# A recurrent attention layer beside a long convolution on one core: who loads the convolution's keys, how far ahead its input is loaded, and in what pieces two weight blocks are fetched

## The chip, the cores and the metric

The kernel runs on one core of one Trainium2 chip. The metric is the device time of one execution in microseconds (us), as the median of several runs. The execution that the profile shows has its own time, given below beside its span.

## The reference

Two independent results are written side by side, each 2048 x 1024. All inputs are bfloat16.

```python
# A: attention over segments of 32 rows, with 8 memory rows that are carried on
mem = mem0                                       # [1, 8, 1024]
for s in range(64):
    h = concat([mem, x[:, 32*s:32*s + 32]], 1)   # 40 rows
    q, k, v = h @ Wq, h @ Wk, h @ Wv             # 32 heads of 128
    p = softmax(where(mask, q @ k^T * scale, -1e9))
    o = (p @ v) @ Wo
    mem = o[:, :8]                               # the next segment waits for this
    outs.append(o[:, 8:])
# B: a state-space layer as a long convolution
K = real(einsum(Cc, exp(dt*A*l), dt*Bc))         # [1024 channels, 2048 steps]
y = irfft(rfft(u padded) * rfft(K padded))[:2048]
b = y.astype(bfloat16) + u * Dskip
return concat([a, b], -1)
```

## The kernel before

The program has three parts in time. The first, up to about 450 us, makes the convolution kernel K and does the work of A that doesn't depend on the memory. K is written to a table Kd in DRAM, the transform of u (the u spectra) to Ud. The second part, from about 450 to 700 us, is the transform: the spectrum of K, its product with that of u, and the inverse. The third is the 64 segments of A, one after the other.

**Transform.** The loop over `b` from 0 to 15 (L1320 to L1357) has one round for each pair of a quarter of the channels (`dq`, 256 channels) and a quarter of the frequencies (`kc`). A round `b`, in the order of its instructions:

- `spectrum(b + 1)` on PE (L1060, 64 matmuls of 256 columns) multiplies the key tiles `KT` with the matrices `MF`. The key tiles for the first two quarters are loaded before the loop; those of the third and fourth (`KT2`) are the deferred ones. ACT copies part of the result (`odd`, L1220 to L1222, tile `osb_`).
- `pointwise(b)` on DVE (L1228 to L1239) combines it with the two tiles `uq` of the u spectrum into `Bt`.
- SyncE issues the loads of the `uq` tiles for round `b + 2` (L1034), then some deferred key loads out of the list `keys` (L1342), then matrices `MI` for the inverse (b below 4), and then, in some rounds, weight blocks of A that are to stay in SBUF (`resident`, 512 KB each).
- From `b` = 4 on, two inverses. `inverse(dq, c)` has 32 matmuls on PE (L1287), with `MI` or with a negated copy `mn` that ACT makes (L1255). ACT scales the result into `yb` (L1303), DVE computes `uu = uu * Dskip + yb` (L1306, L1307), where `uu` is a tile of the input u, and the result is stored by a DMA that ACT issues (L1308), one inverse later.

There are 32 inverses: 24 in the loop, 8 behind it. Each needs one tile `uu` of 128 KB. `load_inverse` issues its load on SyncE; `NIV` is how many inverses ahead that is. `inverses()` calls it after each inverse for the one `NIV` places later. The first `NIV` loads are issued in round 3. Behind the loop, eleven weight blocks, then four blocks for the segments' ring `wst`, then five further weight blocks are issued between the last eight inverses.

Each of SyncE, ACT and GpSimd issues its instructions in program order, DMAs among them. A DMA that has to wait for a buffer or for an earlier DMA holds up what is behind it on its engine.

**Deferred keys.** `load_k` (L995) gathers a key tile from rows of Kd in 31 DMAs. With `later` given, it only appends them to a list, on the queues `qs` in turns. For the two deferred tiles this makes 62 DMAs, mostly of 32 KB in rows of 512 bytes.

**Segments.** Each segment multiplies its 32 rows of state `hT` with all blocks of Wk, Wq, Wv (L365) and then Wo (L475). Most blocks are in SBUF. Twelve are streamed from DRAM copies (WD) in every segment through the four slots of the ring `wst`. Three blocks are kept in PSUM instead, whole or half: `load_kept` copies them there with DVE as 32-bit words (`words`, L292, tile `keep`), and `fetch` copies them back into the tile `arena` in every segment. The block ("k", 0, 7) is kept whole. Of ("q", 0, 7) and ("o", 15), listed in `HALF`, the second half is kept in PSUM, and the first half lies in SBUF (`a_half`, `Whalf`). `load_kept` is called for them within the first segment. In segment 0 the Wo blocks that aren't in SBUF yet are loaded when their turn comes (`unit`).

Of the kernel before, what the change touches and what calls it, by code (L numbers as in the profile page):

```python
# [10 lines left out]
BF16 = mybir.dt.bfloat16  # L11
# [21 lines left out]
SLOTS = 4  # L33
# [199 lines left out]
def part_a(ctx, tc, x, src, WD, HE, seg_len, out_a, ahead, W_res, rest, places, first):  # L233
    nc = tc.nc
# [18 lines left out]
    wst = ahead.wst  # L253
    wres = ctx_w.enter_context(tc.tile_pool(name="a_wres", bufs=1, side="right"))

    loads = [SLOTS]
# [22 lines left out]
    kept, ahead_of, halves = {}, {}, {}  # L279
# [11 lines left out]
    def words(out, in_):  # L291
        nc.vector.tensor_scalar(out=out.bitcast(I32), in0=in_.bitcast(I32), scalar1=0, scalar2=None, op0=ALU.bitwise_or)  # L292

    def stage(key, in_):
        t_ = wst.tile([128, 2048], BF16, name="wst", tag="w%d" % (loads[0] % SLOTS))
        loads[0] += 1
        nc.sync.dma_start(out=t_[:].rearrange("e (h d) -> e h d", h=2) if len(in_.shape) == 3 else t_[:], in_=in_)
        return t_

    def load_kept(key):  # L300
        t_ = first.pop(key) if key in first else stage(key, src(key))
        kept[key] = {}
        for n in (1,) if key in HALF else (0, 1):
            kept[key][n] = ps_k.tile([128, 512], F32, name="keep", tag="keep%d" % sum(len(b) for b in kept.values()))
            words(kept[key][n][:], t_[:, 1024 * n:1024 * n + 1024])
        if key in HALF:
            t_ = ahead.low["half"] if key[0] == "q" else wres.tile([128, 1024], BF16, name="Whalf")
            nc.sync.dma_start(out=t_[:], in_=src(key)[:, 0, :] if key[0] == "o" else src(key)[:, 0:1024])
            halves[key] = [(0, 1024, t_)]

    def fetch(key):

# [334 lines left out]
def part_b(ctx, tc, u, A_re, A_im, B_re, B_im, C_re, C_im, log_dt, Dskip, out_b, ahead, copies, residents, first_state):  # L647
    nc = tc.nc
# [4 lines left out]
    DH, DQ = 512, 256  # L653
    v, sc, gp, pe, sy = nc.vector, nc.scalar, nc.gpsimd, nc.tensor, nc.sync
# [30 lines left out]
    with tc.tile_pool(name="b_par", bufs=1) as par, tc.tile_pool(name="b_parh", bufs=2) as parh, tc.tile_pool(name="b_mg", bufs=2) as mg, \  # L685
# [84 lines left out]
        o = 0  # L770
# [224 lines left out]
    def load_k(d0, n_d, qs, KT, later=None):  # L995
        dsl = slice(d0, d0 + n_d)

        def rows(r0, n, step=1):
            return Kd[r0:r0 + step * (n - 1) + 1:step, dsl]
        n_q = [0]  # L1000

        def get(out, in_):
            q = qs[n_q[0] % len(qs)]
            n_q[0] += 1
            if later is None:
                q.dma_start(out=out, in_=in_)
            else:
                later.append(lambda: q.dma_start(out=out, in_=in_))
        for r in (0, 2, 1, 3):
            k0 = KT[:, 4 * r, :]  # L1010
            get(k0[0:64], rows(r, 64, 4))
            get(k0[64:128], rows(256 + (0, 0, 1, 2)[r], 64, 2))
            k1 = KT[:, 4 * r + 1, :]
            if r == 2:
                get(k1[0:128:2], rows(384, 64, 2))
                get(k1[1:128:2], rows(386, 64, 2))
            else:
                get(k1[:], rows(384 + (0, 0, 0, 1)[r], 128))
            for mc in (2, 3):
                k2 = KT[:, 4 * r + mc, :]  # L1020
                q0 = 512 + 64 * (mc - 2)
                get(k2[0:128:2], rows(q0, 64))
                if r == 0:
                    get(k2[1:128:4], rows(q0, 32, 2))
                    get(k2[3:128:4], rows(q0 + 2, 32, 2))
                else:
                    get(k2[1:128:2], rows(q0 + 1, 64))
        return KT
# [20 lines left out]
    def spectrum(b, s_):  # L1049
        dq, kc = b // 4, b % 4  # L1050
        KN = KNs[dq // 2]
        d = slice(DQ * (dq % 2), DQ * (dq % 2) + DQ)
        KT = ks[0][:, :, d] if dq < 2 else ks[dq - 1][:]
        for half in range(2):
            for r in range(2):
                for cs in range(2):
                    for i, rr in enumerate((r, r + 2)):
                        for mc in range(4):
                            rhs = KN[:, 4 * (rr - 2) + mc, d] if half == 1 and i == 1 else KT[:, 4 * rr + mc, :]
                            pe.matmul(s_[r][half][:, cs, :], lhsT=MF[:, kc, 4 * rr + mc, cs, :], rhs=rhs,  # L1060
                                      start=(i == 0 and mc == 0), stop=(i == 1 and mc == 3), skip_group_check=True)
# [101 lines left out]
    for f in range(-1, 17):  # L1163
        if f == 15:
# [4 lines left out]
            ks = [load_k(0, DH, (sy, gp), ahead.pool.tile([128, 16, DH], BF16, name="KT", tag="kst"))]  # L1169
        if f == 16:  # L1170
            spectra = [load_u(0), load_u(1)]
        for word in ORDER:
            nm, r = word.rstrip("'"), f - word.endswith("'")
            if f == 16 and word == ORDER[0]:
                s0 = ps_e.tile([128, 2, 512], F32, name="pa", tag="pa")
                s1 = [ps_t.tile([128, 512], F32, name="ptt", tag="ptt") for _ in range(2)]
                first = [[s0[:, half, :].rearrange("p (c d) -> p c d", c=2) for half in range(2)],
                         [t_[:].rearrange("p (c d) -> p c d", c=2) for t_ in s1]]
# [25 lines left out]
    iv = ctx.enter_context(tc.tile_pool(name="b_iv", bufs=2))  # L1204
# [9 lines left out]
    KT2 = [pool.tile([128, 16, DQ], BF16, name="KT", tag="KT%d" % i) for i in range(2)]  # L1214
# [23 lines left out]
        for j, op in ((0, ALU.add), (1, ALU.subtract)):  # L1238
            v.tensor_tensor(out=Bt[:, kc, j], in0=Y[:, 0], in1=Y[:, 1], op=op)  # L1239

    NIV = 3
    unsent = []

    def load_inverse(dq, c):
        r, mc = c // 4, c % 4
        uu = iv.tile([128, 2, DQ], BF16, name="uu", tag="uu", bufs=2 * NIV)
        sy.dma_start(out=uu[:], in_=u_v[r][:, mc:mc + 2, DQ * dq:DQ * dq + DQ])
        return uu

# [10 lines left out]
    def inverses(n):  # L1260

        for _ in range(n):
# [3 lines left out]
            inverse(dq, c, nxt.pop(0), *ready.pop(0))  # L1266
            if len(todo) >= NIV:
                nxt.append(load_inverse(*todo[NIV - 1]))

# [20 lines left out]
    def inverse(dq, c, uu, neg, mn):  # L1290
        r, mc = c // 4, c % 4
        d = slice(DQ * dq, DQ * dq + DQ)
        if (dq, c) in early:
            yp = early[dq, c]
            products_back(yp, dq, c, neg, mn, range(3, 4))
        else:
            yp = ps_y.tile([128, 2, DQ], F32, name="yp", tag="yp")[:]
            products_back(yp, dq, c, neg, mn, range(4))
        if todo and not ready:
            ready.append(negated(todo[0][1]))  # L1300
        yb = iv.tile([128, 2, 4, 8, 8], BF16, name="yb", tag="yb", bufs=2)
        for b in range(2):
            sc.activation(out=yb[:, b], in_=yp[:, b, :].rearrange("p (s t e) -> p t s e", s=8, t=4), func=ACT.Copy, scale=float(2.0 / PLEN))  # L1303
        while len(unsent) > (1 if len(todo) > 6 else 0):
            unsent.pop(0)()
        v.tensor_tensor(out=uu[:], in0=uu[:], in1=Dsk[:, d].unsqueeze(1).to_broadcast([128, 2, DQ]), op=ALU.mult)  # L1306
        v.tensor_tensor(out=uu[:], in0=uu[:], in1=yb[:].rearrange("p b t s e -> p b (t s e)"), op=ALU.add)  # L1307
        unsent.append(lambda: sc.dma_start(out=out_v[r][:, mc:mc + 2, d], in_=uu[:]))  # L1308

    keys = []  # L1310
# [9 lines left out]
    for b in range(16):  # L1320
        dq = b // 4
        if b % 4 == 0:
            Bs[dq] = (bp0, bp)[dq % 2].tile([128, 4, 2, 2, 2, DQ], BF16, name="Bt", tag="B")
        if b == 0:
            ks += [load_k(DQ * i, DQ, (sy,), KT2[i - 2], keys) for i in (2, 3)]
        if b == 3:
            nxt = [load_inverse(*todo[n_]) for n_ in range(NIV)]
            pointwise(b, *now)
            ctx_h.close()
            ctx_p.close()  # L1330
            ps_h = ctx.enter_context(tc.tile_pool(name="b_psh", bufs=3, space=PSUM))
            ps_y = ctx.enter_context(tc.tile_pool(name="b_psy", bufs=2, space=PSUM))
        if b + 1 < 16:
            s_ = [ps_h.tile([128, 2, 2, DQ], F32, name="hps", tag="h") for _ in range(2)]
            spectrum(b + 1, [halves(t_) for t_ in s_])
            then = s_[0][:], odd([halves(t_) for t_ in s_])
        if b != 3:
            pointwise(b, *now)
        now = then
        if b + 2 < 16:  # L1340
            spectra.append(load_u(b + 2))
        for _ in range(min(10, len(keys))):  # L1342
            keys.pop(0)()
        if b < 4:
            for i in (2 * b, 2 * b + 1):
                sy.dma_start(out=MI[i][:], in_=MId[2 * i:2 * i + 2].rearrange("c p a k q -> p c a k q"))
        for _ in range({1: 1, 2: 1, 3: 1, 6: 4, 11: 2, 12: 2, 13: 4, 14: 4}.get(b, 0)):
            next(resident)
        if b == 4:
            state = first_state(iv.tile([8, D], BF16, name="m0", bufs=1), iv.tile([128, 8, 24], BF16, name="xt0", bufs=1))  # L1350
            next(state)
        if b == 13:
            state.send(ps_y.tile([128, 8, 128], BF16, name="yp", tag="yp")[:, :, 0:8])
        if b >= 4:
            inverses(2)
        if b == 6:
            negate(ks[1:])  # L1357
# [168 lines left out]
```

## Time and profile before

| | us |
|---|---|
| median of 3 runs | 2073.23 |
| the runs | 2067.98, 2073.23, 2073.27 |
| the profiled execution | 2060.34 |
| its span | 2058.6 |

The span goes from the first to the last instruction on the core. Over it PE is busy 91%, DVE 69%, ACT 51%, GpSimd (POOL) 18%. The mean granted TensorE clock is 0.982. The DMA engines move 590.78 MB, 287 GB/s in the mean. Of the span's time, the chain that ended last lies 35% on PE and 17% on DMA.

In the profile's lines, L1306 is line 1306 of the kernel, `out<-in` names the tiles, and the text in brackets is the time for which the engine was idle before the instruction and what ended that wait. PEld is the weight load of TensorE. An engine's name with a q (SPq, ACTq) is its sequencer, which issues DMAs.

### The profile page before, as it was taken

The numbers are of one execution on the slowest core, as the hardware profiler recorded it, in microseconds if no ns is written. First come the engines' busy times: TensorE is split into PE (matmuls) and PEld (weight loads), VectorE is DVE, ScalarE is ACT, GpSimd is POOL, SyncE is SP. The second block draws the span as 40 slices with busy tenths as digits, with TensorE's granted clock in tenths as the row PEclk, the third lists the DMA queues.
The fourth block names the chain that finished last, engine by engine and source line by source line (L and its number), as shares of the span: only waits on it lengthen the run. The fifth ranks groups of instructions, "written<-read, shape, count | busy, mean of one in ns | idle before, by whom it ended". The sixth has DMA issues, their size and how long they took to land.

```text
span 2058.6 us, 78592 instructions
## 1 busy us (share of the span) xinstructions
PE 1875.7 (91%) x33734; PEld 1190.4 (58%) x33734; DVE 1416.1 (69%) x3352; ACT 1051.5 (51%) x1981; POOL 379.8 (18%) x748
## 2 busy tenths in 40 slices
PE   2699999977999779999999999999999999999999
PEld 1365666656888535555555555555555555555554
DVE  8689989989899346666656656666566666666650
ACT  5899999961333234444444444444444444444430
POOL 2133343353000011111111111111111111111121
PEclk9999999989999879999999999999999999999999
DMA  7697986565736899999999999999999999999991
GB/s 192 177 255 213 261 229 180 157 207 184 228 123 206 311 330 340 341 342 344 344 334 340 340 339 339 347 333 334 338 340 354 344 343 347 339 331 350 333 341 52
DMA packets 351186, 590.78 MB, mean 287 GB/s; under 512 B 108536, under 2 KB 228376, under 8 KB 348788
## 3 DMA queue, kind: packets, MB, share of 16 engines
q1 hardware_dynamic: 297016, 528.00, 75.6%
q10 hardware_dynamic: 44812, 28.26, 4.4%
q0 software_dynamic: 9008, 29.49, 4.3%
q8 instruction: 264, 4.33, 0.8%
q14 instruction: 86, 0.70, 0.1%
HBM read 530.86 MB, written 65.26 MB: 290 GB/s over the span
## 4 chain that ended last, share of the span: by engine, by line
PE 35%; DMA 17%; DVE 1%; issue 1%; ACT 1%; POOL 0%; ACTq 0%; POOLq 0%; DVEq 0%
PE acc L365 20%; PE pp L475 7%; DMA wst<-WD_v 4%; DMA wst<-WD_o 4%; DMA wst<-WD_q 3%; PE pe L611 3%; DMA wst<-WD_k 3%; DMA arena<-PKd 2%; PE tr L376 2%; PE pv L444 1%; DMA out_dram<-arena 1%; PE sc L390 1%; PE pv L448 1%; ACT arena L568 0%; PE sc L394 0%
## 5 line engine op out<-in xcount | busy, mean ns | idle before, releaser
L365 PEld LDWEIGHTS <-a_hT 128*32 128x32 bf16 x12352 | 338.6, 96 | 305.9 <-issue 59.2
L371 ACT CAST arena<-acc 128x512 bf16<-128x512 f32 x384 | 225.1, 586 | 377.0 <-PE acc L365 315.9
L365 PE MATMUL acc<-W,a_hT 128*32 128x512 bf16 x4608 | 375.8, 383 | 0.8 <-issue 0.7
L475 PEld LDWEIGHTS <-arena 128*32 128x32 bf16 x8256 | 212.1, 97 | 93.9 <-issue 45.3
L365 PE MATMUL acc<-wst,a_hT 128*32 128x512 bf16 x2304 | 234.1, 383 | 19.2 <-DMA wst<-WD_v 10.0
L292 DVE TENSOR_SCALAR arena<-keep 128x256 int32<-128x256 int32 (+1 forms) x512 | 176.4, 396 | 42.1 <-PE acc L365 38.0
L379 POOL COPY arena<-arena 128x128 bf16<-128x128 bf16 x128 | 37.6, 294 | 854.1 <-DMA arena<-PKd 316.5
L365 PE MATMUL acc<-MF,a_hT 128*32 128x512 bf16 x2048 | 172.6, 384 | 0.0
L475 PE MATMUL pp<-W_o,arena 128*32 128x256 bf16 x4096 | 138.2, 275 | 7.7 <-DMA W_o<-in_A_Wo_dram 6.3
L414 DVE TENSOR_REDUCE a_mx<-sc 128x4 f32<-128x160 f32 (+1 forms) x192 | 73.1, 381 | 81.8 <-ACT sc L410 81.8
L406 DVE TENSOR_REDUCE a_mx<-sc 128x4 f32<-128x160 f32 (+1 forms) x192 | 72.0, 375 | 82.3 <-PE sc L394 80.6
L167 PE MATMUL pro<-xTl,wsl 128*128 128x512 bf16 x512 | 119.0, 383 | 9.5 <-ACT xTl L111 5.0
L410 ACT ACTIVATE sc<-sc 128x160 f32<-128x160 f32 (+1 forms) x192 | 63.9, 333 | 120.6 <-DVE sc L407 101.3
L1060 PEld LDWEIGHTS <-MF 128*128 128x128 bf16 x1024 | 102.6, 101 | 30.2 <-issue 8.7
L490 DVE COPY arena<-tr 128x512 bf16<-128x512 bf16 x64 | 27.2, 425 | 130.7 <-PE tr L376 130.7
L437 POOL TENSOR_TENSOR arena<-arena,a_BD 128x128 bf16<-128x128 bf16 x128 | 71.1, 555 | 240.1 <-DVE arena L424 221.0
L1060 PE MATMUL hps<-KT,MF 128*128 128x256 bf16 x720 | 94.6, 284 | 14.4 <-DVE x L1229 11.3
L461 ACT CAST arena<-pv 128x256 bf16<-128x256 f32 (+1 forms) x192 | 79.1, 449 | 49.0 <-PE pp L444 39.1
L1287 PE MATMUL yp<-Bt,MI 128*128 128x256 bf16 x680 | 102.9, 273 | 0.8 <-ACT yb L1303 0.8
L568 ACT CAST arena<-pp 128x128 bf16<-128x128 f32 x128 | 27.8, 269 | 141.7 <-PE pp L475 141.7
L1098 ACT ACTIVATE E<-pa 128x648 bf16<-128x648 f32 x128 | 91.4, 714 | 16.9 <-PE pa L1090 9.4
L365 PE MATMUL acc<-W_v,a_hT 128*32 128x512 bf16 x1280 | 93.7, 382 | 0.9 <-issue 0.8
(313 smaller groups left out, 3966.6 us busy)
## 6 DMA issues: line engine op xcount, KB each, us to landing
wst<-WD_v SPq DMA_DIRECT2D x256, 512.0 KB
wst<-WD_k SPq DMA_DIRECT2D x192, 512.0 KB
wst<-WD_o SPq DMA_DIRECT2D x192, 512.0 KB
wst<-WD_q SPq DMA_DIRECT2D x128, 512.0 KB
Ud<-ux POOLq DMA_DIRECT2D x16, 1024.0 KB, 5.5
uq<-Ud SPq DMA_DIRECT2D x32, 512.0 KB
wsl<-in_A_Wk_dram SPq DMA_DIRECT2D x16, 512.0 KB
wsl<-in_A_Wv_dram SPq DMA_DIRECT2D x16, 512.0 KB
```

The lines of the kernel that those rows point to most:

```text
L167: nc.tensor.matmul(a[:], lhsT=w[:, kc, 128 * j:128 * j + 128], rhs=xTl[:, kc, :, :].rearrange("p s k -> p (s k)"), start=(kc == 0), stop=( ...
L292: nc.vector.tensor_scalar(out=out.bitcast(I32), in0=in_.bitcast(I32), scalar1=0, scalar2=None, op0=ALU.bitwise_or)
L365: nc.tensor.matmul(a[32 * g:32 * g + 32, o_:o_ + rhs.shape[1]], lhsT=hT[:, kc, :], rhs=rhs, start=(kc == 0), stop=(kc == KC - 1), tile_pos ...
L371: nc.scalar.copy(out=q, in_=a[:])
L406: nc.vector.tensor_reduce(out=m_, in_=x, axis=AX.X, op=ALU.max)
L414: nc.vector.tensor_reduce(out=m_, in_=x, axis=AX.X, op=ALU.add)
L437: nc.gpsimd.tensor_tensor(out=L[:, 0].rearrange("p (a b) k -> p a b k", a=4), in0=bc(lt[:, :, 0:XL].unsqueeze(2), [128, 4, 4, XL]), in1=bc ...
L461: nc.scalar.copy(out=o[:, i:i + n], in_=p[:, i:i + n, :].rearrange("p a (g q) -> p a g q", g=4))
L475: nc.tensor.matmul(po[32 * qt:32 * qt + 32, o_:o_ + rhs.shape[1]], lhsT=oT[:, h % 4, (h % 16) // 4, :], rhs=rhs, start=False, stop=(h == 3 ...
L1060: pe.matmul(s_[r][half][:, cs, :], lhsT=MF[:, kc, 4 * rr + mc, cs, :], rhs=rhs, start=(i == 0 and mc == 0), stop=(i == 1 and mc == 3), ski ...
L1098: sc.activation(out=T["E", r, e // 4][:, lo:lo + 8 * NE].rearrange("p (i c) -> p i c", i=2), in_=T.pop(("p", r, e))[:, :, 0:4 * NE], func= ...
L1287: pe.matmul(yp[:, b, :], lhsT=m_[:, b, cs, kc, :], rhs=Bt[:, kc, j, half, c_, :], start=(kc == 0 and cs == 0 and half == 0), stop=(kc == 3 ...
```

## The change

It has three parts.

- The deferred key loads are given to SyncE and GpSimd in turns instead of to SyncE alone, and each round takes twelve of them from the list instead of ten.
- `NIV` becomes 6 instead of 3, and the tiles `uu` become nine instead of six.
- `load_kept` treats the half-kept blocks apart. Before, the whole block (512 KB) was loaded into a slot of the ring, its second half copied to PSUM, and its first half loaded a second time (256 KB) into its place in SBUF. Now the second half is loaded into the slot and the first half into its place, 256 KB each.

```diff
     def load_kept(key):
-        t_ = first.pop(key) if key in first else stage(key, src(key))
         kept[key] = {}
         for n in (1,) if key in HALF else (0, 1):
             kept[key][n] = ps_k.tile([128, 512], F32, name="keep", tag="keep%d" % sum(len(b) for b in kept.values()))
-            words(kept[key][n][:], t_[:, 1024 * n:1024 * n + 1024])
         if key in HALF:
-            t_ = ahead.low["half"] if key[0] == "q" else wres.tile([128, 1024], BF16, name="Whalf")
-            nc.sync.dma_start(out=t_[:], in_=src(key)[:, 0, :] if key[0] == "o" else src(key)[:, 0:1024])
-            halves[key] = [(0, 1024, t_)]
+            w = wst.tile([128, 2048], BF16, name="wst", tag="w%d" % (loads[0] % SLOTS))
+            loads[0] += 1
+            h_ = ahead.low["half"] if key[0] == "q" else wres.tile([128, 1024], BF16, name="Whalf")
+            for n, t_ in ((1, w[:, 0:1024]), (0, h_[:])):
+                nc.sync.dma_start(out=t_, in_=src(key)[:, n, :] if key[0] == "o" else src(key)[:, 1024 * n:1024 * n + 1024])
+            words(kept[key][1][:], w[:, 0:1024])
+            halves[key] = [(0, 1024, h_)]
+        else:
+            t_ = first.pop(key)
+            for n in (0, 1):
+                words(kept[key][n][:], t_[:, 1024 * n:1024 * n + 1024])
...
-    NIV = 3
+    NIV, UU = 6, 9
     unsent = []
 
     def load_inverse(dq, c):
         r, mc = c // 4, c % 4
-        uu = iv.tile([128, 2, DQ], BF16, name="uu", tag="uu", bufs=2 * NIV)
+        uu = iv.tile([128, 2, DQ], BF16, name="uu", tag="uu", bufs=UU)
...
         if b == 0:
-            ks += [load_k(DQ * i, DQ, (sy,), KT2[i - 2], keys) for i in (2, 3)]
+            ks += [load_k(DQ * i, DQ, (sy, gp), KT2[i - 2], keys) for i in (2, 3)]
...
-        for _ in range(min(10, len(keys))):
+        for _ in range(min(12, len(keys))):
             keys.pop(0)()
```

## The prediction

> **What bounds the kernel now.** I read the slices of the span first, then the stretches of the transform and of the first segment, then each engine in order of time around the stalls.
>
> From the page, slices of 51.5 us:
>
> ```profile
> PE   2699999977999779999999999999999999999999
> DVE  8689989989899346666656656666566666666650
> PEclk9999999989999879999999999999999999999999
> DMA  7697986565736899999999999999999999999991
> ```
>
> From the fourteenth slice on PE and DMA are both full: these are the 64 segments, and the diff leaves their steady state alone. The change can act only where the string dips: the transform (about 450 to 700 us) and the first segment (699 to 750).
>
> Busy time by stretch (columns: PE, PEld, DVE, ACT, POOL, clock, DMA share, GB/s):
>
> ```profile
> 525.00:550.00 25.00, 22.63 (x208) 20.06 (x206) 17.88 (x19) 10.53 (x16) 0.35 (x1) 1.00 0.70 210
> 550.00:600.00 50.00, 50.00 (x460) 44.79 (x459) 48.59 (x53) 17.58 (x33) 0.00 (x0) 1.00 0.48 152
> 675.00:700.00 25.00, 21.07 (x198) 17.84 (x200) 3.61 (x10) 11.15 (x19) 0.00 (x0) 1.00 0.95 339
> 700.00:725.00 25.00, 16.66 (x249) 7.77 (x238) 11.06 (x28) 7.73 (x14) 1.74 (x4) 0.73 0.88 294
> 725.00:750.00 25.00, 13.39 (x177) 6.38 (x179) 6.50 (x24) 3.17 (x10) 1.10 (x3) 0.60 1.00 368
> ```
>
> From 500 to 675 PE is the bound: 460 matmuls in 50 us are one per 0.109 us. One round (128 of them) takes 14.0 us; DVE needs 13.6 (its first operation of the rounds starts at 537.8, 551.4, 564.9). So a stall of DVE costs only what it makes PE lose. After 700 PE is idle a third to a half of the time, at half clock part of the time, and DMA is the full one.
>
> The stalls in order of time (start, length, engine, line, and in brackets the idle time before and who ended it):
>
> ```profile
> 536.90 0.43 DVE L1306 TENSOR_TENSOR uu<-uu,Dsk 128x512 bf16<-128x512 bf16 x1 [6.74 <-DMA uu<-in_B_u_dram]
> 540.23 0.59 ACT L1220 COPY osb__8141<-hps 128x512 f32<-128x512 f32 x1 [9.21 <-DVE x L1229]
> 543.23 0.28 PE L1287 MATMUL yp<-Bt,mn 128*128 128x256 bf16 x1 [2.37 <-ACT mn L1255]
> 693.22 0.43 DVE L1306 TENSOR_TENSOR uu<-uu,Dsk 128x512 bf16<-128x512 bf16 x1 [8.63 <-DMA uu<-in_B_u_dram]
> 695.75 0.28 PE L1287 MATMUL yp<-Bt,mn 128*128 128x256 bf16 x1 [1.78 <-ACT mn L1255]
> 701.97 0.43 DVE L1306 TENSOR_TENSOR uu<-uu,Dsk 128x512 bf16<-128x512 bf16 x1 [7.79 <-DMA uu<-in_B_u_dram]
> 707.26 1.40 PE L365 MATMUL acc<-arena,a_hT 128*32 128x512 bf16 x4 [6.33 <-DVE arena L292]
> 713.74 0.61 PE L365 MATMUL acc<-a_half,a_hT 128*32 128x512 bf16 x2 [1.99 <-DMA a_half<-in_A_Wq_dram]
> ```
>
> Three times DVE waits for a tile of u, 23.2 us in all; PE loses far less. SyncE's own order says why the tiles are late:
>
> ```profile
> 522.14 11.47 SPq L1008 DMA_DIRECT2D KT<-Kd  x10
> 534.66 0.90 SPq L1247 DMA_DIRECT2D uu<-in_B_u_dram  x2
> ...
> 693.19 0.38 SPq L1247 DMA_DIRECT2D uu<-in_B_u_dram  x1
> ...
> 705.78 0.33 SPq L297 DMA_DIRECT2D wst<-in_A_Wq_dram  x1
> 708.20 0.33 SPq L308 DMA_DIRECT2D a_half<-in_A_Wq_dram  x1
> ```
>
> The first late tile stood behind ten key loads, the later ones behind weight loads of 512 KB: the one issued at 693.19 is used at 701.97.
>
> **The change part by part.**
>
> *u six ahead in nine tiles.* It adds and removes no transfer: 32 loads of 128 KB either way. Six are now issued together at round 3 (three at 508 before). Each later load, issued after inverse n, waits for the store of inverse n-3, before (three ahead, six tiles) as after (six ahead, nine tiles). So SyncE waits for the same stores at the same places; weights queued behind these waits come neither sooner nor later by it. Only the last three such places (inverses 26 to 28) lose their load. Three more 0.4 us issues at round 3 stand before a u-spectrum load that is used 7 us later: nothing. What it gains:
> - At 530 DVE no longer waits 6.74; the ACT copy of 540.23, which waited for DVE's L1229, comes when PE has its data (537.0), mn follows at 538.4, and PE's idle 2.37 goes: **2.4 us**. DVE's other 4 us are worth nothing, since PE is then the only bound and DVE waits for its result each round.
> - At 693 the store behind the late tile held mn in ACT's queue: PE's 1.78 goes, **1.8 us**. PE ends the transform at 694.9 instead of 699.0.
> - The first block of segment 0 waits for copies through PSUM (L292), which wait for the last ACT copy of the inverse (L1303, at 703.44), which stood behind a store waiting for the tile of 701.97. Now that copy comes right after PE's last product, at about 695.2, and the copies start at 695.9. From their start (704.13) to PE's restart (707.26) it was 3.13 us, so PE restarts at 699.0: 8.3 earlier in all, that is **4.1 us** on top of the 4.2. The block itself must have landed: it was issued at 688.99 and a load waiting for its completion went at 695.78; it moves by the same 2.4, to 693.4. In time, with 2 us to spare.
>
> *What DMA takes back.* The next gate is the half block at 713.74, a DMA landing. DMA's work before it: the resident weights, issued from 669.5 on once a store is done, which moves with PE by 2.4. Between 688 and 712 the shares by 4 us are 0.78, 0.94, 1.04, 0.84, 0.99, 0.95 against 1.04 when full: 2.8 us unused (taking 0.94 and 0.99 as they are, 2.0 at least). Fewer bytes before the gate: 0.26 MB (the half block is no longer loaded twice) and three u tiles of 0.13 MB, at 390 GB/s 1.7 us. 2.4 + 2.8 + 1.7 = 6.9: the gate moves to 706.8, not by 8.3. So **minus 1.4 us**.
>
> *Halves once.* Removed: 2 x 256 KB; the DVE copies (4 of 0.69 us) stay, the issues stay four. The first is counted above; the second (for W_o) lies ahead of the burst of W_o loads:
>
> ```profile
> 712.00:716.00 4.00, 2.26 (x21) 0.93 (x21) 0.00 (x0) 1.01 (x2) 0.30 (x1) 0.50 0.60 229
> 740.00:744.00 4.00, 1.81 (x28) 0.85 (x24) 0.00 (x0) 0.00 (x0) 0.00 (x0) 0.50 1.05 390
> ```
>
> The lower row is DMA at its fullest, 390 GB/s; fourteen blocks from 722.3 take until 746, and PE waits for each (11.2 us). The burst begins when PE frees slots, so it moves as a whole; 0.26 MB less before it is **0.7 us** if DMA is behind there, zero if not. The upper row shows that just before it DMA has room, so 0 to 0.7.
>
> *Keys in turns, twelve a round.* 62 loads took SyncE 51.6 us between 478 and 547 (10 in 6.1 to 11.5 us). Now 31 stay, six a round instead of ten: some 25 us of SyncE. GpSimd gets 31; its own key loads at 417 to 431 took 0.53 to 1.1 us each, landing after 3.7. GpSimd is free from 478; nothing there waits by rounds, so it issues 30 of them in 17 to 28 us, and the mask constants (8.5 us, now at 477) follow by about 515; their first reader is after 630. All keys are there by 510 where 544 is needed. Worth on the path: the 1.64 us that ACT waits for KT at 551, not on PE's path, so 0. DVE's own pace beside GpSimd's issues does not change: its 128x1024 operations took 1.22 us at 457 to 478, with such issues, and 1.22 at 490 to 500, without. [...] The row says 11.47 us of SyncE for ten key loads, enough to make a tile late by 6.74; by the row this part alone could have earned the 2.4. [...]
>
> *The clock.* After the 6.33 us idle, PE ran at 0.50 in the stretch 712 to 716, and it stays low until about 720. [...] I take 0 and keep 3 for the range.
>
> Sum: 2.4 + 1.8 + 4.1 - 1.4 + 0.7 = 7.6 us, in a profiled execution of 2060.3 us (span 2058.6). The median of the runs, 2073.2, is 12.9 above it; I carry the difference over: **2065.6 us**.
>
> **The rivals.**
> *DMA returns nearly all.* The weights from 669 to 746 are then one queue, and PE's earlier arrivals meet later landings. For it: share 0.95 to 1.05 in most stretches from 672. Against: 0.60 and 0.78 in two of them. Gain then 2.4 plus 1.3 for 0.52 MB, about 4: 2069.5, within the bound.
> [...]
> *Slower: the key burst.* GpSimd's 30 key loads in rows of 512 bytes share the DMA engines with MI and the u spectra between 478 and 500, where DVE is the bound (24.69 of 25 us busy from 475 to 500). By queue order and bytes I estimate the second half of the spectrum for round 3 lands at 492; DVE reads it at 494.8. Each us beyond these 2.8, in rounds 3 and 4, delays DVE and PE one for one. To end slower by 0.3% it has to cost 13.8 us, a landing 9.7 us late in both rounds. Against: SyncE reaches that load 2 us sooner, and the share there is 0.5 to 0.75. At 10 us in both rounds: 2073.2 - 7.6 + 2 x 7.2 = 2080.
> *The change not doing what it says:* the u tiles stay late only if the store wait moved, and it does not.
>
> **How the numbers follow.** 0.3% is 6.2 us, about what a measurement of this kernel can tell. Main case 0.56: 2062 to 2069, with the doubts of 1.4 and 0.7 and some 2 us between runs (the runs shown lie 5.3 apart), and 0.7 of it beyond the bound. DMA returns it 0.20, a fifth of it beyond the bound by that same scatter. Clock and queue 0.18. Key burst 0.06, nearly all of it slower. Faster: 0.39 + 0.04 + 0.18 = 0.61; slower 0.05; within 0.34. The range 2057 to 2073 takes in the first three cases but for the far end of the third, and leaves the burst out.
>
> **What would show it.** DVE's waits for uu: 23.2 us to under 2; PE's idle at 543 and 695 gone; last inverse product at about 695; first arena product of segment 0 at about 699; a_half product at about 707, still ended by DMA; W_o waits as before, 7 us earlier. Wrong if DVE waits for uq between 490 and 510, or if a_half is used at 710 or later.

## The result, and the profile after

The changed kernel takes 2056.31 us in the median of 22 runs (2043.42 to 2070.85), the kernel before 2071.78 in 22 runs beside it (2057.52 to 2084.58). The ratio is 0.9946, with a 95% interval of 0.9928 to 0.9963: 11.2 us less (7.7 to 14.9). The two medians themselves lie 15.5 us apart; what follows goes by the ratio, to which the interval belongs. The profiled execution took 2056.35 us, its span is 2054.6, its mean clock 0.982. Behind `load_kept` the line numbers are higher by six: L365 is now L371, L475 is L481, L1247 is L1253, L1306 is L1312.

The slices of the page after (51.4 us each):

```profile
PE   2699999977999879999999999999999999999999
DVE  8689989989999436666566666666666666656650
PEclk9999999989999989999999999999999999999999
DMA  7697986676646999999999999999999999999991
```

The strings hardly differ. After the tenth slice PE still dips only in the fourteenth (8 tenths, for 7 before) and the fifteenth (7), where the segments begin. The stretches say more (columns: PE, PEld, DVE, ACT, POOL, clock, DMA share, GB/s):

```profile
525.00:550.00 25.00, 25.00 (x232) 22.40 (x230) 23.48 (x27) 13.16 (x18) 0.34 (x1) 1.00 0.78 248
550.00:600.00 50.00, 50.00 (x461) 44.83 (x459) 47.62 (x50) 16.60 (x32) 0.00 (x0) 1.00 0.40 125
675.00:700.00 25.00, 22.25 (x218) 18.04 (x220) 7.89 (x21) 11.41 (x20) 0.00 (x0) 1.00 1.01 364
700.00:725.00 25.00, 15.96 (x279) 7.76 (x272) 10.29 (x28) 8.54 (x16) 2.08 (x5) 0.85 0.87 313
725.00:750.00 25.00, 17.29 (x262) 8.29 (x265) 5.16 (x18) 4.17 (x11) 1.05 (x3) 0.61 0.94 334
```

In the first row PE has 232 matmuls for 208 before: the hole at 543 is filled. From 550 to 600 nothing has changed, since PE set the pace there before too. From 675 to 700 DMA is full (1.01 for 0.95), and the last row holds some 10 us of segment 1 already, where it held 2 before (262 matmuls for 177).

What DVE waits for at the tile `uu`, SyncE's queue around the second group of loads of it, and PE at the two gates of segment 0:

```profile
its engine sat idle before it (us, times) until:
  ACT yb L1309: 24.3, 19
```

```profile
519.74 5.58 SPq L1014 DMA_DIRECT2D KT<-Kd  x6
...
528.81 2.34 SPq L1253 DMA_DIRECT2D uu<-in_B_u_dram  x2
...
532.21 0.48 SPq L1014 DMA_DIRECT2D KT<-Kd  x1
```

```profile
698.41 1.25 PE L371 MATMUL acc<-arena,a_hT 128*32 128x512 bf16 x4 [1.84 <-DVE arena L292]
705.62 0.61 PE L371 MATMUL acc<-a_half,a_hT 128*32 128x512 bf16 x2 [4.40 <-DMA a_half<-in_A_Wq_dram]
```

No wait for the transfer of `uu` is left; DVE now waits for PE's result, so it is PE that paces the rounds. The arena product came at 707.26 before and comes at 698.41, the product with `a_half` at 705.62 instead of 713.74, and PE's wait there has grown from 1.99 to 4.40 us: the gate was DMA's before and is more so now.

### The profile page after: what moved, and what is told of

Same layout as the page of the kernel before. It is cut to its first block, busy times and chain, and to the rows that moved or that the text cites. A ratio compares the mean times of both kernels' runs of the same rounds, so it can differ in the third digit from the quotient of the medians.

```text
span 2054.6 us, 78607 instructions
## 1 busy us (share of the span) xinstructions
PE 1873.8 (91%) x33734; PEld 1187.8 (58%) x33734; DVE 1413.7 (69%) x3352; ACT 1051.7 (51%) x1981; POOL 398.5 (19%) x778
## 5 line engine op out<-in xcount | busy, mean ns | idle before, releaser
L371 PEld LDWEIGHTS <-a_hT 128*32 128x32 bf16 x12352 | 334.4, 96 | 306.5 <-issue 59.4
L371 PE MATMUL acc<-W,a_hT 128*32 128x512 bf16 x4608 | 371.7, 381 | 1.4 <-issue 1.2
L481 PEld LDWEIGHTS <-arena 128*32 128x32 bf16 x8256 | 212.1, 97 | 98.3 <-issue 47.1
L371 PE MATMUL acc<-wst,a_hT 128*32 128x512 bf16 x2304 | 231.9, 381 | 21.0 <-DMA wst<-WD_v 12.4
L371 PE MATMUL acc<-MF,a_hT 128*32 128x512 bf16 x2048 | 171.3, 382 | 0.0
L481 PE MATMUL pp<-W_o,arena 128*32 128x256 bf16 x4096 | 138.4, 275 | 5.9 <-DMA W_o<-in_A_Wo_dram 5.8
L416 ACT ACTIVATE sc<-sc 128x160 f32<-128x160 f32 (+1 forms) x192 | 63.9, 333 | 120.9 <-DVE sc L413 101.8
L371 PE MATMUL acc<-W_v,a_hT 128*32 128x512 bf16 x1280 | 93.0, 380 | 0.5 <-issue 0.5
```

What stands on the lines that cost most here:

```text
L371: nc.tensor.matmul(a[32 * g:32 * g + 32, o_:o_ + rhs.shape[1]], lhsT=hT[:, kc, :], rhs=rhs, start=(kc == 0), stop=(kc == KC - 1), tile_pos ...
L481: nc.tensor.matmul(po[32 * qt:32 * qt + 32, o_:o_ + rhs.shape[1]], lhsT=oT[:, h % 4, (h % 16) // 4, :], rhs=rhs, start=False, stop=(h == 3 ...
```

## The experiments

Five times in the trace carry the comparison. All are counted from the first spectrum product on PE (at 453.7 to 455.8 in the span): the last inverse product, the first arena product, the a_half product, the last product of segment 0 with the block of Wo in the tile `Whalf` ("last Wo", about half a microsecond before the last of all), and then the time from that product to the end of the span ("rest"). One profiled execution each; the ratios are to the kernel before on the same chip, with the 95% interval.

| kernel | last inverse | arena | a_half | last Wo | rest | ratio |
|---|---|---|---|---|---|---|
| before | 245.4 | 253.6 | 260.1 | 294.3 | 1310.7 | 1 |
| before_again | 244.3 | 252.5 | 259.3 | 291.5 | 1319.0 | |
| half_alone | 251.7 | 260.3 | 266.1 | 298.2 | 1318.6 | 1.0005 (0.9983 to 1.0027) |
| ahead_alone | 246.9 | 251.6 | 260.1 | 294.0 | 1317.4 | 0.9997 (0.9974 to 1.0021) |
| no_keys | 249.3 | 254.0 | 261.1 | 295.2 | 1315.5 | 0.9996 (0.9976 to 1.0016) |
| keys_alone | 241.8 | 248.9 | 256.2 | 288.4 | 1317.4 | 0.9966 (0.9941 to 0.9991) |
| after | 240.5 | 244.2 | 251.4 | 285.8 | 1314.6 | 0.9946 (0.9928 to 0.9963) |
| after_again | 239.7 | 243.0 | 250.3 | 283.2 | 1325.9 | 0.9942 (0.9922 to 0.9961) |
| no_half | 241.6 | 245.2 | 255.8 | 288.4 | 1322.4 | 0.9960 (0.9938 to 0.9983) |
| sp_keys_16 | 249.8 | 253.5 | 261.2 | 294.5 | 1308.2 | |
| gp_keys | 241.8 | 245.2 | 252.7 | 285.5 | 1313.6 | 0.9916 (0.9896 to 0.9937) |
| keys_2of3 | 240.3 | 244.7 | 251.9 | 285.3 | 1306.3 | 0.9945 (0.9926 to 0.9965) |
| late_3 | 239.2 | 242.6 | 249.0 | 283.8 | 1309.3 | 0.9916 (0.9886 to 0.9946) |
| late_2 | 240.0 | 243.4 | 248.7 | 286.2 | 1316.3 | 0.9946 (0.9926 to 0.9967) |

### u six ahead, alone (ahead_alone)

```diff
-    NIV = 3
+    NIV, UU = 6, 9
-        uu = iv.tile([128, 2, DQ], BF16, name="uu", tag="uu", bufs=2 * NIV)
+        uu = iv.tile([128, 2, DQ], BF16, name="uu", tag="uu", bufs=UU)
```

> Only u six ahead in nine tiles; keys and halves as before. Theory (gates in a row: late u, then the kept copies, then the half block's landing): all three waits of DVE for uu are gone (under 2 us in all), PE's idle at 543 and at 694 is gone, the first arena product of segment 0 comes at 698 to 700 (before 707.3), the a_half product at 706.5 to 709 (before 713.7, after 705.6), the last W_o product at 740.5 to 743 (before 747.5, after 739.6). Time 5 to 8 us less than before, ratio 0.996 to 0.9975. Rival A (the queue of SyncE is what made the tiles late, so the keys are needed too): the wait at 537 stays over 3 us and PE's idle at 543 stays. Rival B (a part of the gain of the whole change arises in the steady segments): the last W_o product moves by 7 us here as with the whole change, but the time falls by under 4 us or by over 11.

Measured: DVE's waits for `uu` are gone, as expected, and the arena product follows the last inverse product after 4.8 us instead of 8.2. But the transform isn't shorter at all, and the time is that of before. PE's hole has only moved from 543 to 561. ACT and SyncE in this kernel:

```profile
525.61 12.77 SPq L1008 DMA_DIRECT2D KT<-Kd  x10
...
541.36 8.30 SPq L1008 DMA_DIRECT2D KT<-Kd  x10
...
551.84 1.10 SPq L1008 DMA_DIRECT2D KT<-Kd  x2
```

```profile
547.97 1.91 ACT L1046 ACTIVATE KN<-KT 128x2048 bf16<-128x2048 bf16 x1 [1.55 <-DMA KT<-Kd]
556.95 1.91 ACT L1046 ACTIVATE KN<-KT 128x2048 bf16<-128x2048 bf16 x1 [7.07 <-DMA KT<-Kd]
```

The last of the 62 key loads are issued at 552, the negated copy KN waits 7.07 us for them, and the copy `mn` that PE needs is queued behind KN on ACT (PE's wait for it: 4.1 us). Behind this wait the granted clock is 0.50 from 560.7 to 564.1, and PE does 16 products there, 33 in the 3.4 us after them: so this hole cost more than its 4.1 us.

In the profile of before the same copy waited 1.64 us, and PE did not wait for it:

```profile
550.99 1.91 ACT L1046 ACTIVATE KN<-KT 128x2048 bf16<-128x2048 bf16 x1 [1.64 <-DMA KT<-Kd]
```

So two deliveries were late behind SyncE's key loads: u at 537 and the last keys at 551. With u on time, the keys are what is late, for two reasons. Counted from the first spectrum product, ACT is ready for the copy at 94.7 us, 1.0 to 1.4 us earlier than in the two profiles of before; and the keys let it start at 101.8, 3.0 to 4.5 us later than there (97.3 and 98.8), which is the larger part. In front of the keys SyncE now issues three loads of u more at round 3 (before, then ahead_alone):

```profile
508.12 1.61 SPq L1247 DMA_DIRECT2D uu<-in_B_u_dram  x3
510.78 8.70 SPq L1008 DMA_DIRECT2D KT<-Kd  x10
```

```profile
509.24 3.10 SPq L1247 DMA_DIRECT2D uu<-in_B_u_dram  x6
514.95 7.96 SPq L1008 DMA_DIRECT2D KT<-Kd  x10
```

Counted as above, this group of keys starts at 59.8 us instead of 57.1. How much of the delay the three loads make is not shown: in half_alone, further down, with three loads of u as before, the last keys were issued late too (96.7 us; 93.0 and 93.9 in the two profiles of before, 97.2 here, 99.5 in no_keys). Rival A's sign, PE's idle at 543 as it was, didn't appear, but what it says holds: the keys are needed too.

### Six ahead and the halves, without the keys (no_keys)

```diff
-            ks += [load_k(DQ * i, DQ, (sy, gp), KT2[i - 2], keys) for i in (2, 3)]
+            ks += [load_k(DQ * i, DQ, (sy,), KT2[i - 2], keys) for i in (2, 3)]
-        for _ in range(min(12, len(keys))):
+        for _ in range(min(10, len(keys))):
```

> The whole change without its key part: SyncE alone issues the deferred keys, ten a round. Theory: as with the whole change, since six tiles ahead already take away the late u: DVE's waits for uu under 2 us, arena product at 698 to 700, a_half product at 705 to 707, last W_o product at 739 to 741; ACT again waits 1 to 2 us for KT near 551, off PE's path. Time within 1.5 us of the whole change, ratio to before 0.9935 to 0.9965. Rival A (keys are needed): PE's idle at 543 is back (2 to 3 us) and each later gate 2 to 3 us later, ratio nearer to 0.9965 to 0.998.

The theory missed, and this run confirms the one above. ACT waited for KT not 1 to 2 us but 11.2, and PE twice:

```profile
549.44 1.91 ACT L1052 ACTIVATE KN<-KT 128x2048 bf16<-128x2048 bf16 x1 [4.43 <-DMA KT<-Kd]
558.13 1.91 ACT L1052 ACTIVATE KN<-KT 128x2048 bf16<-128x2048 bf16 x1 [6.77 <-DMA KT<-Kd]
```

```profile
551.40 0.60 PE L1066 MATMUL hps<-KN,MF 128*128 128x256 bf16 x4 [3.22 <-ACT KN L1052]
562.07 0.28 PE L1293 MATMUL yp<-Bt,mn 128*128 128x256 bf16 x1 [2.18 <-ACT mn L1261]
```

The ratio is 0.9996; with the keys it is 0.9946. Two of the three parts, without the keys, bring nothing that can be measured.

### The keys alone (keys_alone)

The reverse of the diff above, on the kernel before.

> Only the deferred key loads in turns, twelve a round; u three ahead in six tiles, half blocks as before. Theory: SyncE's key loads fall from 62 to 31, the wait of DVE for uu at 537 shrinks from 6.74 to under 3 us and PE's idle at 543 goes (2.4 us), but the late tiles at 693 and 702 stay (waits of 7 to 9 us each), so the arena product comes at about 705 (before 707.3), the a_half product at 711 to 714, the last W_o product at 745 to 747.5. Time 0 to 2.4 us less, ratio 0.9988 to 1.000. [...] Rival C (key burst): DVE waits for uq between 490 and 510, and the last inverse product comes later than before (699.0).

The early hole is gone: SyncE has 32 of the 62 loads, GpSimd 30, SyncE's last but one group ends at 524.1, and the late tile is waited for 0.96 us instead of 6.74. The two late tiles at the end stay, and so do the waits behind them (DVE's waits in order of time, then PE's restart):

```profile
531.32 0.42 DVE L1306 TENSOR_TENSOR uu<-uu,Dsk 128x512 bf16<-128x512 bf16 x1 [0.96 <-DMA uu<-in_B_u_dram]
691.25 0.43 DVE L1306 TENSOR_TENSOR uu<-uu,Dsk 128x512 bf16<-128x512 bf16 x1 [9.57 <-DMA uu<-in_B_u_dram]
698.84 0.43 DVE L1306 TENSOR_TENSOR uu<-uu,Dsk 128x512 bf16<-128x512 bf16 x1 [6.64 <-DMA uu<-in_B_u_dram]
```

```profile
704.13 1.40 PE L365 MATMUL acc<-arena,a_hT 128*32 128x512 bf16 x4 [5.18 <-DVE arena L292]
```

The places are as expected; the worth isn't. Segment 0 ends 3.1 to 5.9 us earlier than in the two profiles of before, and the time falls by 7.0 us (1.9 to 12.2) where 0 to 2.4 was expected. Taken by itself this is the only one of the three parts that is shown to gain.

### The half blocks alone, and the whole change without them (half_alone, no_half)

half_alone is the kernel before with the new `load_kept`, no_half the changed kernel with the old one.

> Only the half-kept blocks loaded by halves once; u and keys as before. Theory: the transform does not change (DVE's three waits for uu 20 us or more, arena product at 707 to 708), the a_half product comes 0.3 to 0.8 us earlier than 713.7, the last W_o product 0.5 to 1.5 us earlier than 747.5. Time 0.5 to 1.5 us less, ratio 0.9992 to 0.9998, not to be told from 1 in five rounds. Rival D (DMA has room there, so bytes saved are worth nothing): last W_o product within 0.3 us of before. Rival B (the steady segments gain): ratio under 0.998 although the last W_o product hardly moves.

> The whole change without the half blocks: u six ahead and the keys in turns, the half-kept blocks loaded whole and a half again as before. Theory: transform as with the whole change (239 to 242 us); the a_half product 0.5 to 1.5 us later than with it (251.4 after the first spectrum product), the last W_o product 0.5 to 1.5 us later (285.8). Time 0.5 to 1.5 us more than the whole change, not to be told from it. Rival (the halves are what opened the way for the block behind them): a_half product 3 us later or more.

half_alone doesn't settle its question, because its transform was 6.3 and 7.4 us longer than in the two profiles of before, at a place that the halves don't touch: PE's wait for `mn` at the hole near 543 was 6.79 us there, and the granted clock was 0.50 from 547.7 to 554.5 behind it, with 4.9 us of PE's work at half speed (2.5 us lost, by estimate). Counted from the last inverse product, the a_half product came after 14.4 us, and after 14.7 and 14.9 in the two profiles of before: 0.3 to 0.6 us. no_half missed the other way, as its rival has it (3 us or more):

```profile
711.56 0.61 PE L365 MATMUL acc<-a_half,a_hT 128*32 128x512 bf16 x2 [7.73 <-DMA a_half<-in_A_Wq_dram]
```

The product is 4.4 and 5.5 us later than in the two profiles of the whole change. But SyncE's waits in this execution hold a long one for the landing of a store, in front of weight blocks that stand ahead of the halves in the queue; the longest of this kind in either profile of the whole change is 2.3 us:

```profile
SPq L229 <- DMA out_dram<-uu: 5.1, 1, 5.1
```

So most of it can't be put down to the halves from this one execution. The ratios, 0.9960 and 0.9942 on the same chip, have intervals that overlap. The halves are worth anything from some tenths of a microsecond to some four; what they are worth stays open. So does what u six ahead adds to the keys by itself: no_half, with both, ends segment 0 at the same 288.4 us as keys_alone. The two parts together add 2.6 and 5.2 us to the keys there.

### The kernels before and after once more (before_again, after_again)

> The kernel before, unchanged, profiled once more: how much do its milestones scatter from one execution to the next? Theory (the stall behind SyncE's keys depends on how the key loads happen to run; the first profile of before had a short one): PE's gap near 543 is anything from 2.6 to 7.1 us (7.06 in the run with halves alone, whose transform is the same up to 680), the transform (first spectrum product to last inverse product) 245 to 252 us, the first segment to its last W_o product 46 to 49, the steady rest 1310 to 1319. Rival (the first profile was typical, and the halves made the transform of that run longer): gap 2 to 3.5 us, transform 244.5 to 246.5.

> The whole change, unchanged, once more. Theory (the milestones of the first part are steady where nothing is late, the steady segments scatter by themselves): first spectrum product to last inverse product 239 to 242 us (240.5), to the last W_o product of the first segment 284 to 287 (285.8); the rest to the end anything from 1308 to 1319. No gap of PE over 1.5 us between 500 and 690. Ratio to before 0.992 to 0.9965. Rival (the steady segments gain or lose with the change): the rest lies again within 1 us of 1314.6.

Up to the end of segment 0 the pairs differ by under 3 us: before 294.3 and 291.5, after 285.8 and 283.2 (the last 0.8 less than expected). Of the two expectations for before, the rival (a typical first profile) is the nearer: PE's wait near 543 was 2.84 us, for 2.37 in the first, and the transform took 244.3 us, 0.2 below its range. The 6.79 of half_alone remains a single case. The rest of the span is less steady than expected: 1310.7 and 1319.0 before, 1314.6 and 1325.9 after, and 1306.3 to 1325.9 over all fourteen profiles, with no order by kernel. It is the waits for the streamed blocks that differ; PE's from 800 to 2040 us in the first and the second profile of before:

```profile
PE acc L365 <- DMA wst<-WD_v: 9.8, 15, 2.0
...
PE pp L475 <- DMA wst<-WD_o: 4.7, 10, 0.8
```

```profile
PE acc L365 <- DMA wst<-WD_v: 14.2, 22, 2.2
PE pp L475 <- DMA wst<-WD_o: 8.1, 15, 1.1
```

A single pair of spans (4.0 us apart in the first) therefore says little of an 8 us change; the times up to segment 0's end, and many runs, do.

### Sixteen keys a round on SyncE (sp_keys_16)

```diff
-            ks += [load_k(DQ * i, DQ, (sy, gp), KT2[i - 2], keys) for i in (2, 3)]
+            ks += [load_k(DQ * i, DQ, (sy,), KT2[i - 2], keys) for i in (2, 3)]
-        for _ in range(min(12, len(keys))):
+        for _ in range(min(16, len(keys))):
```

> The whole change, but SyncE alone issues the deferred keys, sixteen a round, so that they end one to two rounds sooner than with ten. Theory (SyncE's issue time, 0.6 to 1.1 us for each of 62 key loads, is the shortage, and something behind them in its queue is always late): ACT's wait of 7 us for KT near 550 is gone, but DVE waits for uq or PE for hps between 490 and 520, 4 us or more in all, the transform takes 246 to 256 us (after 240.5, without the key part 249.3). Rival (only the order was wrong: the keys came last): no new wait over 1 us, transform 240 to 242, as with the whole change.

ACT's wait for KT is gone, and something else is late; DVE's waits:

```profile
498.04 1.23 DVE L1239 TENSOR_TENSOR y<-uq,x 128x1024 f32<-128x1024 f32 x1 [3.44 <-DMA uq<-Ud]
514.26 1.23 DVE L1239 TENSOR_TENSOR y<-uq,x 128x1024 f32<-128x1024 f32 x1 [4.29 <-DMA uq<-Ud]
529.67 0.43 DVE L1312 TENSOR_TENSOR uu<-uu,Dsk 128x512 bf16<-128x512 bf16 x1 [5.73 <-DMA uu<-in_B_u_dram]
```

PE waits 6.82 us for `mn` near 536, and the transform takes 249.8 us, as long as no_keys. With all 62 loads on SyncE, three orders of its queue were run (ten keys a round with three loads of u at round 3, with six of them, and sixteen keys a round), and in each something behind them is late. Over the fourteen profiles the transform takes 244.3 to 251.7 us in the six where SyncE alone issues the deferred keys, and 239.2 to 241.8 in the eight where GpSimd issues some or all. (The span of this execution, 2058.6, is short because its rest is 1308.2.)

### More of the keys on GpSimd (gp_keys, keys_2of3)

The queues are `(gp,)` and `(sy, gp, gp)` instead of `(sy, gp)`.

> The whole change, but GpSimd alone issues all 62 deferred keys, twelve a round. Theory (what counts is that SyncE is rid of enough of them and that KT is whole by 547): SyncE has no wait behind keys, GpSimd's loads end between 520 and 545, DVE does not wait for uu or uq, transform 239.5 to 242 us, all gates as in the whole change, ratio to before 0.993 to 0.9965. Rival (GpSimd takes as long for 62 as SyncE did): the last key is issued after 545, ACT waits for KT over 3 us and PE stalls before hps near 550, transform 243 to 247, ratio 0.996 to 0.999. Rival (key burst on GpSimd slows the u spectra): DVE waits for uq between 490 and 510.

> The whole change with two of three deferred keys on GpSimd (21 stay on SyncE, 41 go), between the whole change (31 and 31) and GpSimd alone (0 and 62). Theory (a queue that issues 62 needs until 547 or later, whichever it is, and what is behind it or reads the last key waits; 41 on GpSimd end at about 527 and 21 on SyncE earlier): no wait of ACT for KT, no wait of DVE for uu or uq, PE without a gap over 0.5 us between 500 and 560, transform 239 to 242 us. Time within 2 us of the whole change. Rival (GpSimd's bursts cost the u spectra or DVE something): DVE waits for uq, or the transform takes over 242 us.

With all 62 on GpSimd the last two are issued at 546.2, behind the mask constants, and ACT waits 4.47 us for KT at 552, as the first rival has it; but PE loses only 0.60 by it. With 41 nobody waits. Neither shows a wait for uq: no cost of the key burst to the u spectra can be seen, not even with all loads on GpSimd. At the end of segment 0 both lie within 0.5 us of the first profile of the whole change, and 2.1 to 2.3 us behind the second. The ratio of 0.9916 for gp_keys is lower, but it is from six runs that weren't taken beside the whole change, and its interval overlaps the other's; no milestone speaks for a gain.

### Weight blocks behind the half block (late_3, late_2)

```diff
-LATE = 5
+LATE = 3
```

> The whole change with two of the five weight blocks that SyncE loads ahead of the q half block put behind it (LATE 3 for 5); no byte more or less. Theory (the a_half gate is the landing order of one DMA queue, at 1.34 us for a block of 512 KB): the a_half product comes 2 to 2.7 us earlier after the first spectrum product than with the whole change (251.4 us there), PE's wait for it falls from 4.4 to 1.5 to 2.5 us, and about half of it is given back in the W_o burst, whose end (285.8 after the first spectrum product) moves by 0 to 2 us. Ratio to before 0.993 to 0.996, not to be told from the whole change. Rival (the gate is not the order, but a completion that the load waits for): a_half product within 0.7 us of the whole change.

> The whole change with three of the five weight blocks put behind the q half block (LATE 2 for 5; with 3 the a_half product came at 249.0 after the first spectrum product, with 5 at 251.4). Theory (landing order at 1.34 us a block, until PE's own arrival is the gate, which is 244.5 to 246.5 after the first spectrum product): a_half product at 247 to 248.3, PE's wait for it 1.5 to 2.5 us; the last W_o product at 282.5 to 284.5 (late_3 283.8), since the blocks moved behind land in the W_o burst. Ratio to before 0.990 to 0.996. Rival (given back in full): last W_o product at 285 or later, as with the whole change.

The a_half product comes nearer. Counted from the last inverse product, it is 10.9 and 10.7 us away in the two profiles of the whole change, 9.8 with two blocks less in front of it (late_3), 8.6 with three (late_2). PE's wait for it is 4.40 and 4.50 us, then 3.57, then 2.45:

```profile
703.00 0.39 PE L371 MATMUL acc<-a_half,a_hT 128*32 128x512 bf16 x2 [3.57 <-DMA a_half<-in_A_Wq_dram]
```

```profile
704.03 0.39 PE L371 MATMUL acc<-a_half,a_hT 128*32 128x512 bf16 x2 [2.45 <-DMA a_half<-in_A_Wq_dram]
```

So the landing order does set this gate, but at half the expected price: 1.0 us for two blocks and 2.2 for three, where 1.34 each was counted. (Of the 2.4 us by which late_3 seems to meet its expectation, 1.3 are a transform that was shorter in that execution.) The last Wo product follows the last inverse product after 45.3 and 43.6 us in the whole change, 44.7 in late_3, 46.1 in late_2: so in late_2 it is given back in full in the burst of Wo loads, as its rival says, though the two profiles of the whole change lie 1.7 us apart themselves. In time late_2 is level with the whole change (0.9946 to 0.9942, same chip). The 0.9916 of late_3 is again from six runs that weren't taken beside it, and its interval holds 0.9942. No version was found that is shown to beat the changed kernel.

## Why the prediction was right, and where it was wrong

Its time, 2065.6 for a median of 2073.2, is a ratio of 0.9963, at the edge of the interval measured. The measured ratio makes 2062.0 us of the 2073.2, in the range of 2057 to 2073; the median of 2056.31 lies just below it, beside a median before of 2071.78. By its own steps, from the two pairs of profiles (before and after, before_again and after_again):

- **The early and the late hole of PE in the transform, 2.4 + 1.8.** The last inverse product is 4.9 and 4.7 us earlier; 4.2 was predicted. PE's waits of 2.37 us at 543 and 1.78 at 696 are gone. By the middle of the transform (600 us) 2.5 and 3.7 us are gained, behind it 2.5 and 1.0: in before_again no wait of PE near 696 is over 0.4 us, so the late hole is there in one execution of the kernel before and hardly in the other.
- **The restart, 4.1 on top.** The arena product follows the last inverse product after 3.7 and 3.4 us, for 8.2 and 8.2 before: 4.5 and 4.8. At 698.41 it is 0.6 us from the predicted 699.0.
- **What DMA takes back, minus 1.4.** The arena product is 9.4 and 9.5 us earlier, a_half 8.7 and 9.0: only 0.7 and 0.5 is taken back. The predicted mechanism, PE waiting longer for a landing, is the one seen (1.99 to 4.40 us).
- **The halves in the Wo burst, plus 0.7.** The last Wo product is 8.5 and 8.3 us earlier, less than a_half's gain; no 0.7 can be seen there. late_2 shows a gain ahead of the burst that isn't carried through it.
- **The sum, 7.6.** By the traces it is 8.4. The 11.2 of the runs has an interval from 7.7 that holds 8.4; for the 2.8 between them no place in the traces was found, and the scatter of the steady segments hides it.
- **The clock, 0, with 3 kept for the range.** No run shows the 3 us. What the traces show is that half clock in segment 0 begins at 703.6 instead of 706.1 and lasts 6.8 us instead of 13.7, before the second stretch of it in the Wo burst, which lasts 20.5 for 23.9; what the shorter stretches are worth in time wasn't separated. Behind the first gap of segment 0, which ends with the arena product at 698.41, the clock stays at 1.00 until 703.6. That isn't so in every run: in keys_2of3, with a gap of 2.90 us there, it is 0.53 in the next 3.6 us (last section).

**The step that failed** is the price of the keys, 0: the sum has 2.4 us for the early hole, put down to six tiles ahead alone. Six ahead doesn't take it without the keys. ahead_alone and no_keys gain nothing in the transform, since the keys are late next, and keys_alone gains 7.0 us by time. The prediction had the sign before it, ACT's wait of 1.64 us for KT at 551, and read it as harmless because it was off PE's path; in ahead_alone this wait is 7.07 us and on it. A small part of that is that PE and ACT come 1.0 to 1.4 us earlier with u on time; the larger is that the last keys come 3.0 to 4.5 us later. The three loads of u more at round 3, which the prediction put at "nothing", looking only at the u spectrum behind them, stand in front of these keys. So of two deliveries that are late behind one queue, the second one's slack has to be counted anew with the first one cured. That the sum came out right is luck in this: the real change has all three parts, and the 2.4 was counted once. As a forecast of the change without the keys the same steps would have been wrong (0.9996 measured, 0.9976 to 1.0016).

Taken one by one the key loads are short to issue: one takes SyncE 0.59 us in the median (before), and the ones that GpSimd issued landed after 4.8 us in the median (after). What made u and the last keys late is the sum over one queue. The prediction's 51.6 us (the rows add up to 51.5) aren't all issue time either: the 62 issues take 34.3 us, and most of the rest is SyncE waiting between two key loads for the landing of earlier transfers (us in all, times, longest):

```profile
SPq L1008 <- DMA uq<-Ud: 6.9, 8, 1.5
SPq L1008 <- DMA W_k<-in_A_Wk_dram: 3.4, 3, 1.3
SPq L1008 <- DMA MI<-MId: 2.2, 3, 1.4
SPq L1008 <- DMA out_dram<-uu: 2.2, 1, 2.2
```

In the profile after, the rows of the deferred keys on SyncE add up to 26.4 us, of which the 32 issues take 19.0 and such waits 6.3. So the part saved some 15 us of issuing and 8 of waiting in the queue; what each is worth wasn't separated. "All keys are there by 510" was also off: SyncE's last went at 532.2 and GpSimd's at 517.5, in time for 545.6, where KN reads them. And by the slices PE and DMA are both full from the sixteenth on, not the fourteenth; nothing in the sum hangs on it.

The rivals: DMA didn't return nearly all (8.4 is left at segment 0's end). The key burst didn't come, not even with 62 loads on GpSimd. "Clock and queue", at 0.18, stood for a gain of 12.6 us by the author's estimate, in which the clock's 3 us are shown by no run. The time alone, whose interval ends at 14.9, can't exclude such a gain; by the traces up to segment 0's end it is not what happened: 8.4 is gained there, and the clock is 0.50 for 6.8 us from 703.6 on.

## What to carry to other kernels

When a transfer is late, add up the time that its queue spends on everything in front of it, issues and waits, and then ask what else lies behind the same work: here, curing one delivery by asking for it earlier handed the lateness to the next, while taking work off the queue cured both. Price the parts of a change together and each without the others, since a part that looks free may be what lets another gain. And with a long steady part that scatters by 20 us from one execution to the next, judge a change of 8 us by the times at the stages it touches, not by two spans.

## What the runs showed of the hardware

**Half clock followed a gap of PE of 2.90 us and not one of 3.12 us.** In keys_2of3 the gap of 2.90 us (between the starts of two matmuls) was followed by a granted clock of 0.53 from 698.80 to 702.40, in before_again the one of 3.12 us by 1.00 (columns as above; the gap is in the second row of the first fence and in the first of the second):

```profile
692.00:695.50 3.50, 3.50 (x45) 2.62 (x46) 0.72 (x2) 0.00 (x0) 0.00 (x0) 1.00 1.04 409
695.50:698.80 3.30, 0.79 (x16) 0.18 (x8) 2.08 (x5) 0.66 (x2) 0.00 (x0) 1.00 1.05 414
698.80:702.40 3.60, 3.59 (x32) 2.30 (x34) 1.02 (x4) 0.59 (x1) 0.00 (x0) 0.53 1.06 395
```

```profile
542.50:545.60 3.10, 0.32 (x3) 0.03 (x1) 3.07 (x4) 2.94 (x5) 0.00 (x0) 1.00 0.48 145
545.60:549.00 3.40, 3.34 (x31) 3.01 (x32) 3.33 (x4) 1.50 (x4) 0.00 (x0) 1.00 0.68 174
```

The stretches at half clock that end within the span lasted 3.4, 6.8, 10.2, 13.7 and 23.9 us in before, and 3.4, 6.8, 10.2 and 20.5 us in after. So in these runs the length of the gap alone doesn't tell whether half clock follows; what else decides it wasn't tried.

**GpSimd's mask constants took 7.9 to 10.1 us behind deferred key loads, 3.1 to 4.2 where SyncE issues those.** The same twelve small selects took 3.13 us at 478 in before, 7.92 at 506 in after, 10.14 at 534 in gp_keys; over the fourteen profiles 3.1 to 4.2 us at 478 to 481, where SyncE alone issues the keys, and 7.9 to 10.1 at 506 to 534 in the others. They lie off the path here, but two key loads stood behind them in gp_keys. What slowed them wasn't tried.

**Loads on SyncE waited for the landing of a store that ACT issued:** 5.1 us in no_half, at the weight blocks of L229, which go to other tiles than the one that is stored, and 2.2 us in before, at a key load. What joins the two is a semaphore: in the records of before the key load issued at 530.60 and ACT's store issued at 526.93 tell of their landing through the same one (106), and the load waits for it first. SyncE's and ACT's transfers share eight of them in before and after (101 to 103 and 105 to 109), GpSimd's have eight of their own (110 to 117). SyncE's waits between its key loads, above, are for transfers into other tiles too.
